# A token-mixing kernel: the last 64 tokens' products in pairs in the array's halves, and the bias on GpSimd

## The chip, the cores and the metric

The kernel runs on one core of a Trainium2 chip. The metric is the device time of one execution in microseconds (us). The engines are TensorE (PE in the profile; PEld is its loading of weights), VectorE (DVE), ScalarE (ACT), GpSimd (POOL) and SyncE (SP, which here only issues DMAs).

## The reference

Attention with pooled keys and values feeds a residual MLP block that first mixes tokens and then channels. Batch 8, 8 heads, 576 tokens, head size 64, so 512 channels:

```
k_p, v_p = means of k, v over groups of 8 tokens          # 72 of each
attn     = softmax(q k_p^T / 8) v_p                       # per batch and head, 576 x 64
x        = the heads side by side                         # 576 x 512
a1       = alpha1 * x + beta1
u        = x + lam * (w_tok a1)                           # w_tok 576 x 576: the "mix"
out      = u + lam * (relu((alpha2*u + beta2) w_ch1) w_ch2)
```

The mix is linear, so lam * (w_tok a1) is a product of w_tok with xs = lam*alpha1*x, plus a bias: the sum of each row of w_tok times lam*beta1.

## The kernel before

Tokens are cut in five chunks. Chunks 0 to 3 hold tokens 0 to 511 (token 4p+c is in partition p of chunk c); the last 64 tokens are the fifth, "chunk 4", and those of an even and an odd batch share one 128-partition chunk. All 36 chunks stand in a list in which four make a block of the MLP: nine blocks, n = 0 to 8. While PE works on the MLP of block n, the attention and the mix of batch n+1 are put between its products. The order on every engine is written out by hand: each step goes into the list `todo` with a place in time (`at`), the list is sorted, and the steps are issued in that order. Places 0 to 15 of a block are `mlp_A` (L838: first channel product, with a Relu on ACT), 16 to 31 the second product (`mlp_B` in blocks 0 and 1; from block 2 on `product`, L945, a Strassen-like form with seven products of half size, whose sums of operands are `hidden_sum`, L931, on DVE, and whose results `gather`, L976, adds up on DVE).

For each batch: `att_S4` (L689) makes the scores, with 64-row products in pairs in the array's two halves, and `exp` (L722) their exponentials on ACT into `ET`, whose last 64 columns beyond the tokens are kept at 1. `att_AV` (L733) multiplies by the values, and DVE divides (L749) and scales (L751) into `x_tm`, `x` for short, five columns of 128 tokens by 64 channels. Of the fifth, for the last 64 tokens, an even batch uses partitions 0 to 63 and an odd one 64 to 127. `att_X` (L761) multiplies by lam*alpha1 for two heads at a time into `xs_pool`, in bf16: four columns at L765, and the half column of the last tokens at L758 (`rest_X`). It runs on DVE, but for heads 4 and 5 on GpSimd.

`mix_T` (L794) makes one chunk of the mix with five products of 512 columns, four over 128 tokens each and one over the last 64 tokens. The bias is in that fifth product: row 64 of `xs` holds lam*beta1 and row 64 of the weights `wtT` the row sums of w_tok (odd batches: row 0, with the tokens in rows 64 to 127, and weights moved to column 5 of `wtT` by `setup_wtok_odd`). Chunk 4 of an odd batch makes both batches' last tokens, ten products with 64 columns of weights, in the array's column halves. DVE adds x (L805), ACT makes a bf16 copy (L809), and `mix_uT` (L813) transposes it by a DMA on SP's queue for the MLP.

PSUM is shared by two pools: `gp` (L218), six banks in turn, and two banks `ch`. GpSimd also sums keys (`sum_k`, L368), casts (`cast_rem`, L351) and issues some loads. What decides places around the mix, in batch b of block n = b-1:

```
at = 21.5 + 0.9 * c + 0.7 * (c == 4) if first else 21.0 + (1.3 if b == 2 else 1.15) * c
when = ((3, (4.6, 14.6)), (1, (8.6, 18.86)), (2, (8.8, 18.98)), (4, (22.3, 23.0)))   # hidden_sum
```

Of the kernel before, what the change touches and what calls it, by code (L numbers as in the profile page):

```python
# [188 lines left out]
def direct(  # L189
# [255 lines left out]
    for i in range(4):  # L445
        if i < 2:
            t = const.tile([SPG, 4, 66], F16, tag=f"vp1_{i}", name=f"vp1_{i}")
            nc.vector.memset(t, 8.0)
            vp1_pool.append(t)
            t = const.tile([P, 2, 4, SPG], BF, tag=f"kpT_{i}", name=f"kpT_{i}")  # L450
            nc.vector.memset(t, 0.0)
            kpT_pool.append(t)
            kp_pool.append(const.tile([P, 4, SPG], BF, tag=f"kp_{i}", name=f"kp_{i}"))
# [68 lines left out]
    def setup_rowsum(tcx):  # L522

        trc = P if tcx < 4 else REM
        cols = slice(P * tcx, P * tcx + trc)
        ps = gp("ps_rs")
        for sc in range(5):
            nc.tensor.matmul(out=ps[:, 0:trc], lhsT=ones_bf if sc < 4 else ones_lo,  # L528
                             rhs=wtT[:, sc, cols], start=(sc == 0), stop=(sc == 4))
        nc.scalar.copy(out=wtT[64:65, 4, cols], in_=ps[64:65, 0:trc])  # L530

    def setup_wtok_odd():
        nc.vector.memset(wtT[0:64, 5, 0:S], 0.0)
# [155 lines left out]
    def att_S4(b, u):  # L689

        st = st1[b]
        qT, kp, rest = st["qT"][u], kp_pool[u], st["rem_qT"]
        lo = [psB.tile([P, DM], FP, tag="ch", bufs=2, name="ps_s") for _ in range(2)]
        hi = [gp("ps_s") for _ in range(2)]
        r = [gp("ps_r")[0:SPG, 0:128].rearrange("p (h i) -> p h i", i=64) for _ in range(2)]

        def main(i):
            for a in range(2):
                rows = slice(64 * a, 64 * a + 64)
                nc.tensor.matmul(  # L700
                    out=(hi if i > 1 else lo)[a][0:SPG, 256 * (i % 2):256 * (i % 2) + 256],
                    lhsT=kp[rows, i, :], rhs=qT[rows, 2 * i:2 * i + 2, :])

        def rests(i):
            for a in range(2):
                rows = slice(64 * a, 64 * a + 64)
                nc.tensor.matmul(  # L707
                    out=r[a][:, i // 2], lhsT=kp[rows, i + a, :],
                    rhs=rest[rows, :, 2 * u + i // 2::4].rearrange("p c i -> p i c"))
# [12 lines left out]
        def exp(k):  # L722
            if k < 2:
                o, i = ET[:, k::2, 512:S], r[k]
            else:
                a, (pair, h) = k % 2, pairs[k // 2 - 1]
                o = ET[:, h:h + 2, 256 * a:256 * a + 256]
                i = pair[a][0:SPG, :].rearrange("p (h i) -> p h i", i=256)
            nc.scalar.activation(out=o, in_=i, func=AF.Exp, bias=0.0, scale=0.125)  # L729

        st["exp", u] = exp

    def att_AV(b, h):  # L733
        st = st1[b]
        if "x" not in st:
            st["x"] = st1[b - 1]["x"] if b % 2 else work.tile([P, 6, DM], FP, tag="x_tm", bufs=1, name="x_tm")
        ET, vp1, x = st["ET"][h], vp1_pool[h // 4], st["x"]
        ps_av = gp("ps_av")
        av = ps_av[:, 0:5 * 66].rearrange("p (c x) -> p c x", x=66)
        odd = b % 2  # L740
        for c in range(4):
            m0 = 256 * (c % 2) + 128 * (c // 2)
            nc.tensor.matmul(out=av[:, odd + c, :], lhsT=ET[:, m0:m0 + 128],  # L743
                             rhs=vp1[:, h % 4, :])

        r0 = 512 - 64 * odd
        nc.tensor.matmul(out=av[:, 4 - 4 * odd, :], lhsT=ET[:, r0:r0 + 128], rhs=vp1[:, h % 4, :])  # L747
        rec = recs[:, 8 * b + h]
        nc.vector.reciprocal(out=rec, in_=av[:, :, 64:65])  # L749
        dd = D * h  # L750
        nc.vector.tensor_tensor(out=x[:, 1 - odd:6 - odd, dd:dd + D], in0=av[:, :, 0:64],  # L751
                                in1=rec.unsqueeze(2).to_broadcast((P, 5, D)), op=ALU.mult)
# [8 lines left out]
    def att_X(b, h0, h1, eng=nc.vector, rest=True):  # L761

        x, xs = st1[b]["x"], xs_pool[b % 2]
        cols = slice(D * h0, D * h1)
        eng.tensor_tensor(  # L765
            out=xs[:, 0:4, cols], in0=x[:, 1:5, cols],
            in1=lamal_bc[:, cols].unsqueeze(1).to_broadcast((P, 4, D * (h1 - h0))), op=ALU.mult)
        if rest:
            rest_X(b, h0, h1, eng)
# [18 lines left out]
    def keep_warm(count):  # L788

        ps = psB.tile([P, DM], FP, tag="ch", bufs=2, name="ps_warm")  # L790
        for _ in range(count):
            nc.tensor.matmul(out=ps, lhsT=warm[:, 0:P], rhs=warm)  # L792

    def mix_T(b, c, eng=nc.vector):  # L794
        key, s = chunk_of(b, c)
        ps_tok = gp("ps_tok")
        parts = ((b % 2, 0, P),) if c < 4 else ((0, 0, 64), (1, 64, P))
        for sc in range(5):
            for i, p0, p1 in parts:
                kk, at = (P, sc) if sc < 4 else (P, 5) if i else (65, 4)  # L800
                nc.tensor.matmul(out=ps_tok[p0:p1], lhsT=wtT[0:kk, at, P * c:P * c + p1 - p0],  # L801
                                 rhs=xs_pool[i][0:kk, sc, :], start=(sc == 0), stop=(sc == 4))
# [95 lines left out]
    def scale_w2(g, i):  # L898

        if g not in w2l:  # L900
            if g == 1:
                both = const.tile([P, 6 * DM], BF, tag="vecs", name="w2_l")
                w2l[1] = both[:, 0:4 * DM].rearrange("p (i d) -> p i d", d=DM)
                wino["spare"] = both[:, 4 * DM:].rearrange("p (j t) -> p j t", t=HALF)
            else:
                w2l[g] = const.tile([P, 4, DM], BF, tag=("wt_bf", None, "w2_0", "w2_1")[g],
                                    name="w2_l")
        nc.vector.tensor_tensor(out=w2l[g][:, i], in0=w2[g][:, i], in1=lam_bc, op=ALU.mult)

# [166 lines left out]
    def attention(b):  # L1076
# [22 lines left out]
        for u in range(2):  # L1099
            at = (9.0 if first else 6.3, 13.6)[u]  # L1100
            todo.append((at, lambda u=u: att_S4(b, u)))
            for k, dt in enumerate((0.1, 0.1, 0.1, 0.7, 1.7, 1.75) if u else (0.1, 0.1, 0.1, 1.1, 2.1, 3.1)):
                todo.append((at + dt, lambda u=u, k=k: st1[b]["exp", u](k)))
            early = (5.7, 6.2, 4.2, 4.7) if first else (5.7, 6.2, 2.9, 3.4)
            for i, dt in enumerate((2.9, 3.4, 4.6, 5.1) if u else early):
                h = 4 * u + i
                todo.append((at + dt, lambda h=h: att_AV(b, h)))
                if i % 2:
                    eng = nc.gpsimd if h == 5 or first and h < 5 else nc.vector
                    todo.append((at + dt + 0.1, lambda h=h, eng=eng: att_X(b, h - 1, h + 1, eng)))  # L1110
        if first:
            for i, u in enumerate((0, 2, 1)):
# [4 lines left out]
            for i, at in enumerate(((0.2, 1.4, 2.2), (5.0, 7.2, 8.0))[u]):  # L1117
                todo.append((at, lambda u=u, i=i: att_V(b, u, 4 >> i)))
        for c in range(5):
            at = 21.5 + 0.9 * c + 0.7 * (c == 4) if first else 21.0 + (1.3 if b == 2 else 1.15) * c  # L1120
            if c < 4 or b % 2:
                todo.append((at, lambda c=c: mix_T(b, c)))
                key = (b, c) if c < 4 else (b - 1, 4)
                todo.append((at + (1.0 if first else 1.8), lambda key=key: mix_uT(key)))
        return todo

    for n in range(NBLK):
# [26 lines left out]
                todo.append((1.2 + g, lambda g=g: weight_sum(4, g)))  # L1154
        if n >= FIRST:
            last = n == NBLK - 1
            when = ((3, (4.6, 14.6)), (1, (8.6, 18.86)), (2, (8.8, 18.98)), (4, (22.3, 23.0)))
            if last:
                when = ((3, (4.6, 12.6)), (1, (8.6, 16.1)), (2, (8.8, 16.2)), (4, (18.6, 19.6)))
            for i, at in when:  # L1160
# [17 lines left out]
            else:  # L1178
                for m in range(4):
                    todo.append((27.2 if m < 2 else 29.2, lambda m=m: store(n, m)))  # L1180
        if n == 0:
            todo.append((6.2, lambda: setup_rowsum(4)))
            todo.append((8.3, setup_wtok_odd))
            for g in range(2, 4):
# [66 lines left out]
```

## Time and profile before

| what | value |
|---|---|
| median of 3 runs | 332.6 us (332.5 to 332.74) |
| the profiled execution | 332.3 us, span 330.6 us |
| granted TensorE clock | 1.000 |
| PE busy | 324.9 us, 98% |
| DVE, ACT, POOL busy | 235.5 us, 175.5 us, 95.6 us |
| the mix's products (L801) | 200, busy 44.9 us |
| starts of blocks 1 to 8 on PE | 67.55, 102.76, 137.68, 171.30, 206.21, 239.83, 274.74, 300.78 us |
| POOL's wait for x ahead of L765 | 108.6 us in 8 waits |

The span is the time from the first to the last instruction; the time beside it has 1.7 us more. A product is shown as rows x columns of the array that its weights take (64\*72 is half of the rows), then the rows and columns of what moves through. A record of a product lasts longer than its stream, so the times from start to start tell what a product costs PE. An even batch's block takes 33.6 us, an odd one's 34.9.

### The profile page before, as it was taken

How to read it: one execution, taken by the hardware profiler on the slowest of the kernel's cores; microseconds unless marked ns; L12 is line 12 of the kernel's file. 1: busy time of each engine (PE TensorE's matmuls, PEld its weight loads, DVE VectorE, ACT ScalarE, POOL GpSimd, SP SyncE). 2: the span in 40 equal slices, each digit the busy share in tenths (PEclk: the TensorE clock that was granted, in tenths of full speed). 3: DMA queues.
4: the chain of work that ended last, by engine and by line, in shares of the span. 5: the costliest groups of instructions: out<-in, count | busy, mean ns of one | idle time of the engine just before them, and what ended most of it. 6: DMA issues, size and time to landing. Idle time of an engine off the chain costs nothing.

```text
span 330.6 us, 6522 instructions
## 1 busy us (share of the span) xinstructions
PE 324.9 (98%) x2528; PEld 208.9 (63%) x2528; DVE 235.5 (71%) x490; ACT 175.5 (53%) x322; POOL 95.6 (29%) x110
## 2 busy tenths in 40 slices
PE   8999999999999999999999999999999999999995
PEld 3667764455545576656775677557755866586584
DVE  6674389999589969776967796878688783265263
ACT  2775989458323852387128812782268225803710
POOL 8769738301256011700290028102610200000000
PEclk9999999999999999999999999999999999999999
DMA  8999999959894982499549934995340044003003
GB/s 119 193 219 270 268 210 249 207 145 124 165 255 68 221 203 59 76 227 165 164 119 201 171 125 89 207 195 157 65 136 2 0 65 143 2 0 129 2 32 97
DMA packets 66618, 45.83 MB, mean 139 GB/s; under 512 B 34541, under 2 KB 57205, under 8 KB 66586
## 3 DMA queue, kind: packets, MB, share of 16 engines
q1 hardware_dynamic: 52236, 32.67, 42.6%
q0 software_dynamic: 13824, 12.40, 22.9%
q8 instruction: 20, 0.33, 0.4%
q10 hardware_dynamic: 526, 0.34, 0.3%
q14 instruction: 12, 0.10, 0.1%
HBM read 38.30 MB, written 9.44 MB: 144 GB/s over the span
## 4 chain that ended last, share of the span: by engine, by line
PE 98%; DVE 1%; issue 0%; ACT 0%
PE ps_h L849 38%; PE ps_w L972 26%; PE ps_tok L801 12%; PE ps_ch L869 8%; PE ps_av L743 3%; PE ps_s L700 2%; PE ps_warm L792 2%; PE ps_kp L632 1%; PE ps_r L707 1%; PE ps_av L747 1%; PE ps_q L589 1%; PE ps_sc L680 0%; PE ps_rs L528 0%; PE ps_w L516 0%; PE ps_uT L825 0%; PE ps_v L659 0%
## 5 line engine op out<-in xcount | busy, mean ns | idle before, releaser
L849 PE MATMUL ps_h<-u_fm,w 128*128 128x512 bf16 (+2 forms) x608 | 133.7, 369 | 0.2 <-DVE bias_cols L852 0.2
L856 ACT ACTIVATE H<-ps_h,bias_cols 128x512 bf16<-128x512 f32 x144 | 98.1, 688 | 56.5 <-PE ps_h L849 55.5
L849 PEld LDWEIGHTS <-w 128*128 128x128 bf16 x608 | 65.8, 114 | 49.7 <-issue 2.2
L972 PEld LDWEIGHTS <-H 128*128 128x128 bf16 x560 | 53.4, 98 | 10.9 <-DVE u_sb L990 1.2
L809 ACT CAST u_bf<-u_sb 128x512 bf16<-128x512 f32 x32 | 19.8, 618 | 70.0 <-issue 39.9
L972 PE MATMUL ps_w<-w_l,H 128*128 128x256 bf16 x448 | 53.6, 273 | 0.0
L990 DVE TENSOR_TENSOR u_sb<-u_sb,ps_w 128x512 f32<-128x512 f32 x54 | 36.3, 682 | 17.0 <-PE ps_w L972 17.0
L765 POOL TENSOR_TENSOR xs<-x_tm,lamal_bc 128x512 bf16<-128x512 f32 x12 | 15.9, 1330 | 108.8 <-DVE x_tm L751 108.6
L801 PE MATMUL ps_tok<-xs,wtT 128*128 128x512 bf16 (+3 forms) x200 | 44.9, 381 | 0.1
L805 DVE TENSOR_TENSOR u_sb<-x_tm,ps_tok 128x512 f32<-128x512 f32 (+1 forms) x40 | 27.3, 683 | 9.9 <-PE ps_tok L801 9.9
L751 DVE TENSOR_TENSOR x_tm<-ps_av,recs 128x320 f32<-128x320 f32 x64 | 31.5, 492 | 2.6
L729 ACT ACTIVATE ET<-ps_s 72x512 f16<-72x512 f32 x56 | 32.3, 591 | 0.0
L801 PEld LDWEIGHTS <-wtT 128*128 128x128 bf16 (+3 forms) x200 | 17.4, 100 | 16.2 <-issue 1.1
L749 DVE RECIPROCAL recs<-ps_av 128x5 f32<-128x5 f32 x64 | 12.1, 188 | 16.7 <-PE ps_av L747 16.6
L670 DVE TENSOR_TENSOR v_u<-v_u 72x1024 f32<-72x1024 f32 (+1 forms) x24 | 22.7, 948 | 0.2
L972 PE MATMUL ps_w<-w_t,h_s 128*128 128x256 bf16 x168 | 22.6, 273 | 0.0
L869 PEld LDWEIGHTS <-H 128*128 128x128 bf16 x128 | 11.9, 98 | 13.7 <-issue 0.4
L372 POOL TENSOR_TENSOR k_raw<-k_raw 128x512 f32<-128x512 f32 x14 | 18.7, 1338 | 1.2 <-PE ps_ch L869 0.7
L972 PEld LDWEIGHTS <-h_s 128*128 128x128 bf16 x168 | 16.4, 98 | 4.1
L941 DVE TENSOR_TENSOR H<-H,H 128x1024 bf16<-128x1024 bf16 x14 | 9.7, 690 | 12.8 <-ACT H L856 12.7
L374 POOL TENSOR_TENSOR k_bf<-k_raw 128x512 bf16<-128x512 f32 x14 | 18.5, 1318 | 1.1
L743 PEld LDWEIGHTS <-ET 72*128 72x128 f16 x256 | 14.0, 97 | 6.0 <-DVE vp L664 0.3
(153 smaller groups left out, 369.3 us busy)
## 6 DMA issues: line engine op xcount, KB each, us to landing
out_dram<-u_sb SPq DMA_DIRECT2D x29, 256.0 KB
k_raw<-in_k_dram SPq DMA_DIRECT2D x12, 512.0 KB
v_u<-in_v_dram SPq DMA_DIRECT2D x12, 512.0 KB
q_bf<-in_q_dram POOLq DMA_DIRECT2D x16, 256.0 KB, 7.4
w<-in_moe_w_ch_dram POOLq DMA_DIRECT2D x6, 512.0 KB, 12.9
out_dram<-u_sb SPq DMA_DIRECT2D x11, 128.0 KB
w<-in_moe_w_ch_dram POOLq DMA_DIRECT2D x1, 1024.0 KB, 14.3
k_raw<-in_k_dram POOLq DMA_DIRECT2D x2, 512.0 KB, 16.7
```

Source lines behind the costliest of these rows:

```text
L670: nc.vector.tensor_tensor(out=out, in0=t[:, :, 0:width], in1=t[:, :, width:2 * width], op=ALU.add)
L729: nc.scalar.activation(out=o, in_=i, func=AF.Exp, bias=0.0, scale=0.125)
L743: nc.tensor.matmul(out=av[:, odd + c, :], lhsT=ET[:, m0:m0 + 128], rhs=vp1[:, h % 4, :])
L751: nc.vector.tensor_tensor(out=x[:, 1 - odd:6 - odd, dd:dd + D], in0=av[:, :, 0:64], in1=rec.unsqueeze(2).to_broadcast((P, 5, D)), op=ALU.mult)
L801: nc.tensor.matmul(out=ps_tok[p0:p1], lhsT=wtT[0:kk, at, P * c:P * c + p1 - p0], rhs=xs_pool[i][0:kk, sc, :], start=(sc == 0), stop=(sc == 4))
L805: nc.vector.tensor_tensor(out=s["u"][p0:p1, :], in0=x[p0:p1, 1 + c if c < 4 else 5 - 5 * i, :], in1=ps_tok[p0:p1, 0:DM], op=ALU.add)
L809: nc.scalar.copy(out=s["u_bf"], in_=s["u"])
L849: nc.tensor.matmul(out=ps_h[:, t0:t1 + one], lhsT=w1_of(cc, j), rhs=rhs, start=(cc == 0), stop=(cc == 3))
L856: nc.scalar.activation(out=H4[n, j // 4][:, j % 4, :], in_=ps_h, func=AF.Relu, bias=bias_cols[:, j:j + 1], scale=1.0)
L869: nc.tensor.matmul(out=ps, lhsT=H_of(n, j)[:, 128 * m:128 * m + 128], rhs=(w2l if n else w2)[j // 4][:, j % 4, :], start=(j == 0), stop=(j ...
L972: nc.tensor.matmul(out=ps, lhsT=stat(j), rhs=moving(j), stop=(j == 7), start=(first and (pp == 0 or alone) and j == 0), skip_group_check=True)
L990: nc.vector.tensor_tensor(out=o, in0=o, in1=banks[key, "both"], op=ALU.add)
```

## The change

For the third batch on (b > 1; the first two stay as they are):

- `exp` writes the exponentials of the last 64 tokens twice, so `att_AV` gives them in both halves of the partitions, and `att_X` multiplies all five columns in one instruction of 640 elements per partition, on DVE for all heads.
- Chunks are mixed by `mix_in_pairs`. The products over the last 64 tokens of two chunks (0 and 1, 2 and 3) are issued together ahead of the first one's other products, one in rows 0 to 63 of the array and one in rows 64 to 127, each into its own bank. In chunk 4 the two batches' such products take rows 0 to 63 by columns 0 to 63 and rows 64 to 127 by columns 64 to 127.
- No bias is in the products. `bias_x` (row sums of w_tok times lam*beta1, bf16, for 128 channels at a time) is made once in block 0: five reductions on DVE (`sum_wtok`), one product `ps_row` that spreads lam*beta1 over the partitions, and twenty scaled copies on ACT (`setup_bias_x`). After `att_X` GpSimd adds it to x in place: one instruction of 640 for even batches, one of 512 and one of 128 for odd.
- Places move: the mix's chunks to 21.8 + 1.1 c (b = 2: 21.4 + 1.2 c), which puts chunks 2 to 4 one product later, `hidden_sum` 1's second half from 18.86 to 16.6, ahead of head 5, and `hidden_sum` 2's from 18.98 to 21.6, behind three gathers.
- Tiles are shared anew to make room for `bias_x`.

```diff
+    def sum_wtok(c):
+        p1 = P if c < 4 else REM
+        nc.vector.tensor_reduce(out=sums[0:p1, c:c + 1], in_=wt_bf[0:p1, S * c:S * c + S],
+                                op=ALU.add, axis=AX.X)
+        if c == 4:
+            nc.sync.dma_start(out=sums[64:128, 4:5], in_=sums[0:64, 4:5])
+    def setup_bias_x(hp, c):
+        if not ps_row:
+            ps_row.append(gp("ps_row"))
+            nc.tensor.matmul(out=ps_row[0], lhsT=ones_bf[64:65], rhs=xs_pool[0][64:65, 4, :])
+        if c == 0:
+            bias_x.append(wino["spare0"] if hp == 3 else const.tile(
+                [P, 5, 2 * D], BF, tag=("kpT_0", "kpT_1", "vs16")[hp], name="bias_x"))
+        nc.scalar.activation(out=bias_x[hp][:, c], in_=ps_row[0][:, 2 * D * hp:2 * D * hp + 2 * D],
+                             func=AF.Copy, bias=0.0, scale=sums[:, c:c + 1])
...
-            if k < 2:
+            if k < 2 and b < 2:
                 o, i = ET[:, k::2, 512:S], r[k]
+            elif k < 2:
+                o = ET[:, k::2, 512:].rearrange("p h (n i) -> p h n i", i=64)
+                i = r[k].unsqueeze(2).to_broadcast((SPG, 2, 2, 64))
...
-        r0 = 512 - 64 * odd
+        r0 = 512 if b > 1 else 512 - 64 * odd
...
+        if b > 1:
+            x = x[:, 1 - b % 2:6 - b % 2, cols]
+            eng.tensor_tensor(
+                out=xs[:, :, cols], in0=x, op=ALU.mult,
+                in1=lamal_bc[:, cols].unsqueeze(1).to_broadcast((P, 5, D * (h1 - h0))))
+            bias = bias_x[h0 // 2]
+            for x, bias in ((x[:, 1:5], bias[:, 0:4]), (x[:, 0:1], bias[:, 4:5])) if b % 2 else (
+                    (x, bias),):
+                nc.gpsimd.tensor_tensor(out=x, in0=x, in1=bias, op=ALU.add)
+            return
...
+    def mix_in_pairs(b, c, parts):
+        if c % 2 == 0:
+            for k in range(2):
+                i, p0, p1 = parts[k] if c == 4 else parts[0]
+                cc = c if c == 4 else c + k
+                if k == 0 or c < 4:
+                    mixed[b, cc] = gp("ps_tok")
+                rows = slice(64 * k, 64 * k + 64)
+                nc.tensor.matmul(out=mixed[b, cc][p0:p1],
+                                 lhsT=wtT[rows, 4 + k, P * cc:P * cc + p1 - p0],
+                                 rhs=xs_pool[i][rows, 0 if i else 4, :], start=True, stop=False)
+        for sc in range(4):
+            for i, p0, p1 in parts:
+                nc.tensor.matmul(out=mixed[b, c][p0:p1], lhsT=wtT[:, sc, P * c:P * c + p1 - p0],
+                                 rhs=xs_pool[i][:, sc + i, :], start=False, stop=(sc == 3))
...
-                    eng = nc.gpsimd if h == 5 or first and h < 5 else nc.vector
+                    eng = nc.gpsimd if first and h < 6 else nc.vector
...
-            at = 21.5 + 0.9 * c + 0.7 * (c == 4) if first else 21.0 + (1.3 if b == 2 else 1.15) * c
+            at = (21.5 + 0.9 * c + 0.7 * (c == 4) if first else
+                  21.4 + 1.2 * c if b == 2 else 21.8 + 1.1 * c)
...
-            when = ((3, (4.6, 14.6)), (1, (8.6, 18.86)), (2, (8.8, 18.98)), (4, (22.3, 23.0)))
+            when = ((3, (4.6, 14.6)), (1, (8.6, 16.6)), (2, (8.8, 21.6)), (4, (22.3, 23.0)))
...
+            for c in range(5):
+                todo.append((8.35 + 0.1 * c, lambda c=c: sum_wtok(c)))
+                for hp in range(4):
+                    todo.append((26.3 + hp + 0.2 * c, lambda hp=hp, c=c: setup_bias_x(hp, c)))
```

More of the change, by code (lines that the diff above doesn't have):

```diff
@@ L449, in direct @@
             vp1_pool.append(t)
-            t = const.tile([P, 2, 4, SPG], BF, tag=f"kpT_{i}", name=f"kpT_{i}")
+            t = const.tile([P, 640], BF, tag=f"kpT_{i}", name=f"kpT_{i}")
+            t = t[:, 0:8 * SPG].rearrange("p (a h g) -> p a h g", a=2, h=4)
             nc.vector.memset(t, 0.0)
@@ L530, in setup_rowsum @@
         nc.scalar.copy(out=wtT[64:65, 4, cols], in_=ps[64:65, 0:trc])
+    sums = const.tile([P, 5], FP, tag="sums", name="sums")
+    bias_x = []
+    def sum_wtok(c):
[4 more added lines that the diff above has]
+            nc.sync.dma_start(out=sums[64:128, 4:5], in_=sums[0:64, 4:5])
+    ps_row = []
+    def setup_bias_x(hp, c):
[7 more added lines that the diff above has]
+                             func=AF.Copy, bias=0.0, scale=sums[:, c:c + 1])
     def setup_wtok_odd():
@@ L792, in keep_warm @@
             nc.tensor.matmul(out=ps, lhsT=warm[:, 0:P], rhs=warm)
+    mixed = {}
+    def mix_in_pairs(b, c, parts):
[13 more added lines that the diff above has]
+                                 rhs=xs_pool[i][:, sc + i, :], start=False, stop=(sc == 3))
     def mix_T(b, c, eng=nc.vector):
         key, s = chunk_of(b, c)
-        ps_tok = gp("ps_tok")
         parts = ((b % 2, 0, P),) if c < 4 else ((0, 0, 64), (1, 64, P))
[L798 to L802, printed above, removed]
+        if b > 1:
+            mix_in_pairs(b, c, parts)
+            ps_tok = mixed.pop((b, c))
+        else:
+            ps_tok = gp("ps_tok")
+            for sc in range(5):
+                for i, p0, p1 in parts:
+                    kk, at = (P, sc) if sc < 4 else (P, 5) if i else (65, 4)
+                    nc.tensor.matmul(out=ps_tok[p0:p1],
+                                     lhsT=wtT[0:kk, at, P * c:P * c + p1 - p0],
+                                     rhs=xs_pool[i][0:kk, sc, :], start=(sc == 0), stop=(sc == 4))
         for i, p0, p1 in parts:
@@ L904, in scale_w2 @@
                 wino["spare"] = both[:, 4 * DM:].rearrange("p (j t) -> p j t", t=HALF)
+            elif g == 0:
+                both = const.tile([P, 5 * S + 64], BF, tag="wt_bf", name="w2_l")
+                w2l[0] = both[:, 0:4 * DM].rearrange("p (i d) -> p i d", d=DM)
+                wino["spare0"] = both[:, 4 * DM:4 * DM + 640].rearrange("p (c d) -> p c d", c=5)
             else:
-                w2l[g] = const.tile([P, 4, DM], BF, tag=("wt_bf", None, "w2_0", "w2_1")[g],
+                w2l[g] = const.tile([P, 4, DM], BF, tag=(None, None, "w2_0", "w2_1")[g],
                                     name="w2_l")
```

## The prediction

> **What bounds the kernel now.** I read the page's busy shares and chain first, then what TensorE (PE) waited for, then the timeline of PE at the places that the change touches, then VectorE (DVE) just ahead of the mix.
>
> ```profile
> PE 324.9 (98%) x2528; PEld 208.9 (63%) x2528; DVE 235.5 (71%) x490; ACT 175.5 (53%) x322; POOL 95.6 (29%) x110
> PE 98%; DVE 1%; issue 0%; ACT 0%
> ```
>
> ```profile
> PE ps_warm L792 <- DVE early L413: 1.4, 1, 1.4
> PE ps_h L849 <- DVE bias_cols L852: 0.2, 1, 0.2
> ```
>
> PE is busy throughout and is the whole chain; its waits add up to 1.6 us, all ahead of 30 us. So only fewer PE microseconds can win, and no later wait is there to be removed. Other engines matter where they come late for PE.
>
> What does a product in half the array cost? The scores' products (L700, L707) already run in such pairs. Timeline of PE in the block of the fifth batch (b=4):
>
> ```profile
> 151.12 0.60 PE L849 MATMUL ps_h<-u_fm,w 128*128 128x512 bf16 x2
> 151.65 0.30 PE L700 MATMUL ps_s<-qT,kp 64*72 64x256 bf16 x2
> ...
> 151.85 0.39 PE L700 MATMUL ps_s<-qT,kp 64*72 64x256 bf16 x4
> 152.08 0.24 PE L707 MATMUL ps_r<-rem_qT,kp 64*72 64x64 bf16 x2
> 152.15 0.28 PE L700 MATMUL ps_s<-qT,kp 64*72 64x256 bf16 x2
> 152.36 1.92 PE L849 MATMUL ps_h<-u_fm,w 128*128 128x512 bf16 x8
> ```
>
> Unbroken, a whole-array product of 512 columns takes 0.216 us (five mix products from 159.98 to 161.06) and one of 256 takes 0.109 (eight L972 from 161.06 to 161.93). Four half-array products of 256 take 0.23 us (151.85 to 152.08), so the halves do run two at once. But at both borders PE loses time with nothing to wait for. Two L849 products from 151.12 end at 151.55; the first half starts 0.10 later. The last two halves start at 152.15, stream 0.107, and the next product starts at 152.36: 0.10 lost. The eight after it take 1.76 until the next line at 154.12, against 1.73: the first after a border costs 0.03 more. Borders into and out of the mix's 64-column products show the same:
>
> ```profile
> 200.54 1.04 PE L972 MATMUL ps_w<-w_t,h_s 128*128 128x256 bf16 x8
> 201.50 1.27 PE L801 MATMUL ps_tok<-xs,wtT 128*64 128x512 bf16 x10
> 202.71 1.05 PE L972 MATMUL ps_w<-w_l,H 128*128 128x256 bf16 x8
> ```
>
> Eight of 0.109 end at 201.41, the next starts at 201.50; ten products in column halves then take five streams (1.08) plus 0.12 until 202.71.
>
> **The change, part by part.** The sum is made on the profiled execution: 332.3 us (span 330.6, 1.7 around it); the median shown is 332.6, 0.3 above it, and I add the sum to the median.
>
> *Pairs.* Each batch from the third on has two pairs (chunks 0/1 and 2/3), 12 in six batches. A pair replaces two products (0.432) by: border 0.10, first-after-border 0.03, one stream 0.216, border back 0.10, first product after it 0.03: 0.476. Net +0.04, not -0.216. Six second pairs: +0.25. (The first pairs are with the wait, below.)
>
> The Trainium skill (TensorEngine Tiling (Array Packing), Key Properties) says that a change of tiling mode drains TensorE. The trace agrees, with 0.10 us at each border. By that page's Theoretical Speedup (twice for a contraction of 64 or less) the 12 pairs would save 2.6 us.
>
> *Chunk 4* (odd batches, three of them). Before, its last-token products were already two at once, in column halves. Now they are in two quarters (64 rows by 64 columns), followed by the eight in column halves: nothing saved, and one border more, 0.13 each, if quarters-to-halves counts as a border. No row shows that: below 0.13 down to 0 if it doesn't; up to 0.35 if the two quarters, which write one bank, also go one after the other (0.216). I take 0.13, since every change of shape in the trace costs it: +0.39.
>
> The Trainium skill (same page, Gotcha 1: PSUM Pressure) says that different row tiles can't access one PSUM bank at the same time. That would give the 0.35, +0.65 over three batches; no run here shows it.
>
> *ps_row.* One more 512-column product with one row, in block 0: 0.10+0.03+0.216+0.10+0.03 = +0.48; between 0.22 (no borders) and 0.52.
>
> *The wait at the mix.* Before, GpSimd (POOL) multiplied heads 4-5 (L765) and DVE only 6-7, then came `hidden_sum` 1. Odd batch b=5:
>
> ```profile
> 188.97 0.20 DVE L749 RECIPROCAL recs<-ps_av 128x5 f32<-128x5 f32 x1 [1.52 <-PE ps_av L747]
> 189.27 0.49 DVE L751 TENSOR_TENSOR x_tm<-ps_av,recs 128x320 f32<-128x320 f32 x1
> 190.00 0.19 DVE L749 RECIPROCAL recs<-ps_av 128x5 f32<-128x5 f32 x1 [0.24 <-PE ps_av L747]
> ...
> 191.03 0.19 DVE L749 RECIPROCAL recs<-ps_av 128x5 f32<-128x5 f32 x1 [0.31 <-PE ps_av L747]
> ...
> 192.41 0.74 DVE L765 TENSOR_TENSOR xs<-x_tm,lamal_bc 128x512 bf16<-128x512 f32 x1
> 193.18 0.29 DVE L758 TENSOR_TENSOR xs<-x_tm,lamal_bc 64x128 bf16<-64x128 f32 x1
> 193.50 0.69 DVE L941 TENSOR_TENSOR H<-H,H 128x1024 bf16<-128x1024 bf16 x1
> ```
>
> ```profile
> 193.60 0.38 PE L801 MATMUL ps_tok<-xs,wtT 128*128 128x512 bf16 x1
> ```
>
> PE reaches the mix at 193.60; the first four parts of xs are done at 193.15, a margin of 0.45. The instruction order of the changed program puts two more things on DVE in this stretch: `hidden_sum` 1 (0.60 from start to start) between heads 4 and 5, and the multiplication for heads 4-5. The new multiplications are 640 wide: 0.74 plus a quarter of a 72x512 step (1.21-0.68 = 0.53 more for 512) = 0.87. DVE's chain: scale 4 at 189.27, hidden sum 189.68, division 5 190.28, scale 190.50 to 190.99, xs(4-5) 191.03, division 6 191.78, scales to 193.12, xs(6-7) 193.15 to 194.02, handed over by 194.05. The first pair needs the fifth part, so all of it. PE waits 0.45, with all its later work queued behind. The same working gives 0.34 in the even batches b=4, 6 (xs at 160.27, PE there at 159.98) and 0.20 for b=2 (no hidden sum there; 89.95 against 89.80). Sum 3 x 0.45 + 2 x 0.34 + 0.20 = 2.23. The border into the first pair lies inside this wait, so that pair is 0.376 against 0.432: -0.34 for six. Net +1.89. Bounds: 0, if DVE were 0.45 quicker than worked out; +3.0 more (five batches by 0.6), if the hidden sum meets POOL: the like-typed L929 ran 1.30 us with POOL beside it and 0.68 without. I take neither: POOL's add for heads 2-3 should be over by 188.7, a microsecond before the hidden sum.
>
> *At nothing.* POOL's bias adds: about 1.27 + 0.45 us (its L765, L758) four times a batch, in POOL's idle 17.3 us ahead of 190.80; the last runs from 194.05 to 195.9, while DVE has three gathers and a hidden sum (2.4 us) ahead of the first `u` addition, so DVE doesn't wait. Behind the adds on POOL queue `cast_rem` and `sum_k`, done 4.5 us before their products; uncovered, each lost microsecond would be one of PE. Five reductions on DVE in block 0: 0.49 at 320 wide, by slope some 0.7 start to start at 576, 3.5 in all, in DVE's idle 3.50 ahead of 39.82 (and one small DMA on SP, idle there); uncovered, they would delay that cast, which scores at 44.33 need. Twenty ACT copies: 0.17 start to start, 3.5 us, in ACT's idle 3.07 ahead of 68.62; the first Relu is 0.5 late, covered by PE's six banks (0.86 us each). Exponentials of 256 instead of 128 columns: +0.2 us per four heads, in ACT's 0.18 waits. The chunks mixed one product later reach the transposes on SP's queue some 1.5 us later, with `att_Frem` now ahead of one (1.2 us); the tightest, 132.38 for 137.68, keeps over 3 us; 0 to 1 us in one block.
>
> Sum: 0.25 + 0.39 + 0.48 + 1.89 = +3.0; 332.6 + 3.0 = 335.6, forecast 335.5.
>
> **The rivals.**
> - *Halves without borders* (faster). If a lone pair cost one stream: 12 x 0.216 = 2.6 saved, 0.22 for ps_row, no waits: 330.2. For it: halves start together. Against: 0.10 at every border in the trace. It decides where a round trip costs under 0.216; the rows say 0.26.
> - *One border hidden, no wait.* 0.13 a pair: -1.0, +0.35 for ps_row, +0.2 for chunk 4: 332.1, the same. Against: both sides are seen.
> - *Borders, but no wait at the mix.* All 12 pairs +0.5, chunk 4 +0.39, ps_row +0.48: 334.0. For it: 0.45 us is small, and DVE's idle 0.24 and 0.31 between heads may absorb more than I counted.
> - *A worse meeting.* The hidden sum beside POOL's adds (half of 3.0) or quarters one after the other (+0.65): 336.2 to 338.6. For it: L929's 1.30.
>
> **How the numbers follow.** Forecast 0.55 (335.5), no wait 0.17, worse 0.15, same 0.07, faster 0.06. Faster by over 0.2% (0.7 us, about what this kernel's measurement can tell) 0.06, within it 0.07, slower 0.87. The range runs from the no-wait case with chunk 4 at its low end (333.5) to one part of the worse case (337.3).
>
> **What would show it.** In the changed profile: PE gaps of 0.10 on both sides of each 64x512 pair, starts 0.13 apart behind chunk 4's quarters, a PE wait of 0.2 to 0.5 on DVE's xs ahead of each batch's first pair, some 0.5 around ps_row, and L929-like long hidden sums only if POOL meets them. Pairs followed at once by the next product would prove me wrong, as would a first pair that finds xs ready.

## The result, and the profile after

The changed kernel takes 336.98 us (median of 5 runs, 336.39 to 338.03) against 332.54 us (332.29 to 332.74): ratio 1.0138, 95% interval 1.0117 to 1.0159. The forecast was 335.5, range 333.5 to 337.3. So the sign was right and the size was 1.5 us short. The profiled execution is the longest of the five (338.03 us, span 336.3), which matters below. Single executions, of the kernel before too, had a granted clock of 0.98 to 0.995 instead of 0.997 to 1.000 and took 1 to 4 us longer; they are the high ends of the ranges of ten and twelve runs below.

The page's busy shares and its chain, after the change:

```profile
PE 323.9 (96%) x2498; PEld 206.7 (61%) x2529; DVE 243.5 (72%) x483; ACT 182.3 (54%) x342; POOL 122.4 (36%) x134
PE 76%; DVE 13%; DMA 3%; ACT 3%; POOL 2%; issue 2%; POOLq 0%; ACTq 0%; DVEq 0%
```

PE's busy time, as recorded, has not grown, but PE is no longer the whole chain: VectorE stands in it with 13%. (31 of PE's product records are missing here, as the counts 2498 and 2529 show; a place where two starts lie 0.43 instead of 0.216 apart, with nothing to wait for, is such a hole.) What PE waits for, longest first:

```profile
PE ps_tok L843 <- DVE xs L795: 1.9, 6, 0.4
...
PE ps_s L725 <- DVE x_tm L779: 0.7, 1, 0.7
...
PE ps_r L732 <- ACT H L918: 0.3, 1, 0.3
```

The first line is the wait that the prediction named, in all six batches. The wait for `x_tm` (L779) and the one for ACT's Relus (L918) were not in its sum. The mix of the batch whose VectorE lines the prediction showed (b=5), VectorE first, then PE:

```profile
193.44 0.68 DVE L1007 TENSOR_TENSOR H<-H,H 128x1024 bf16<-128x1024 bf16 x1
...
194.78 0.82 DVE L795 TENSOR_TENSOR xs<-x_tm,lamal_bc 128x640 bf16<-128x640 f32 x1
...
196.89 1.01 DVE L795 TENSOR_TENSOR xs<-x_tm,lamal_bc 128x640 bf16<-128x640 f32 x1
```

```profile
194.81 2.79 PE L1038 MATMUL ps_w<-w_l,H 128*128 128x256 bf16 x24
197.96 0.39 PE L843 MATMUL ps_tok<-xs,wtT 64*128 64x512 bf16 x2 [0.37 <-DVE xs L795]
...
201.76 1.04 PE L1038 MATMUL ps_w<-w_t,h_s 128*128 128x256 bf16 x8
202.73 0.39 PE L843 MATMUL ps_tok<-xs,wtT 64*128 64x512 bf16 x2
203.06 1.04 PE L848 MATMUL ps_tok<-xs,wtT 128*128 128x512 bf16 x4
```

The hidden sum (L1007) and both 640-wide multiplications stand in VectorE's row as worked out, and the last ends at 197.90. PE's 24 products end their streams at 197.43; the first pair starts at 197.96, 0.53 later. The border into it lies inside this wait: in `whole_rows` below, where there is no border, the first product waits just as long. The second pair waits for nothing: eight products from 201.76 end at 202.63, the pair starts at 202.73 and the next product at 203.06 (0.10, one stream of 0.216, 0.11), and the product after that comes 0.01 later than without a border. That is 0.43 in all. Two whole-array products take 0.432. The pair gains nothing.

Where the time went can be added up without any hole in the records from ScalarE's 144 Relus, since both kernels have the same ones in the same order. The table gives, for every traced kernel, by how much PE's work falls behind the profile of before in each stretch (difference of a Relu's start to that of the same Relu before the change, and of that again from stretch to stretch), us:

| kernel | to the first Relu | blocks 0 and 1 | mix b=2 | each mix b=3, 5, 7 | each mix b=4, 6 | end | span in all |
|---|---|---|---|---|---|---|---|
| changed | +0.20 | +2.65 | +0.17 | +0.55 | +0.27 | +0.54 | +5.73 |
| `bias_early` | -0.35 | +1.47 | +0.17 | +0.55 | +0.27 | +0.41 | +3.91 |
| `hidden_back` | +0.03 | +1.93 | +0.17 | +0.35 | +0.07 | +0.18 | +3.51 |
| `one_trip` | +0.13 | +1.58 | +0.21 | +0.33 | +0.06 | +0.13 | +3.16 |
| `whole_rows` | +0.17 | +1.58 | +0.29 | +0.54 | +0.38 | +0.42 | +4.84 |
| `scale_later` | +0.06 | +0.43 | +0.17 | +0.55 | +0.27 | +0.43 | +3.29 |
| `no_add_b2` | -0.39 | +1.09 | +0.06 | +0.57 | +0.27 | +0.83 | +3.84 |
| `attx_pool` | -0.05 | +1.92 | -0.03 | +0.11 | -0.03 | +0.41 | +2.53 |
| `all_mended` | +0.38 | +0.22 | +0.20 | +0.02 | -0.15 | +0.89 | +1.46 |
| `all_mended_x` | -0.34 | +0.27 | +0.01 | -0.22 | -0.24 | +0.03 | -1.18 |
| `mended_again` | -0.23 | +0.70 | +0.00 | -0.22 | -0.24 | +0.02 | -0.65 |
| `no_row` | +0.09 | +4.46 | +0.01 | -0.22 | -0.24 | +0.05 | +3.45 |

The first and the last column are start-up loads and the landing of the last stores; they differ by up to 0.9 between kernels whose code there is alike, so they are taken as the spread of single executions. The mix columns repeat to 0.01. The mixes cost 2.36 in all (0.17 + 3 x 0.55 + 2 x 0.27) where the prediction had 2.53. Blocks 0 and 1 cost 2.65 where it had 0.48. There lies the miss.

### The profile page after: what moved, and what is told of

It is laid out like the page before. It is cut to its first block, busy times and chain, and to the rows that moved or that the text cites. A ratio compares the mean times of both kernels' runs of the same rounds, so it can differ in the third digit from the quotient of the medians.

```text
span 336.3 us, 6525 instructions
## 1 busy us (share of the span) xinstructions
PE 323.9 (96%) x2498; PEld 206.7 (61%) x2529; DVE 243.5 (72%) x483; ACT 182.3 (54%) x342; POOL 122.4 (36%) x134
## 4 chain that ended last, share of the span: by engine, by line
PE 76%; DVE 13%; DMA 3%; ACT 3%; POOL 2%; issue 2%; POOLq 0%; ACTq 0%; DVEq 0%
PE ps_h L911 34%; PE ps_w L1038 19%; PE ps_tok L848 7%; PE ps_ch L931 5%; DVE x_tm L779 4%; DVE xs L795 3%; DMA wt_bf<-in_moe_w_tok_dram 3%; PE ps_s L725 2%; PE ps_tok L862 2%; DVE w_l L974 2%; PE ps_tok L843 2%; PE ps_av L771 1%; DVE recs L777 1%; ACT bias_x L554 1%; ACT H L918 1%
## 5 line engine op out<-in xcount | busy, mean ns | idle before, releaser
L918 ACT ACTIVATE H<-ps_h,bias_cols 128x512 bf16<-128x512 f32 x144 | 97.7, 696 | 45.0 <-PE ps_h L911 44.0
L801 POOL TENSOR_TENSOR x_tm<-x_tm,bias_x 128x640 f32<-128x640 f32 (+2 forms) x27 | 28.7, 1075 | 89.8 <-DVE xs L795 83.2
L779 DVE TENSOR_TENSOR x_tm<-ps_av,recs 128x320 f32<-128x320 f32 x64 | 31.5, 492 | 2.3
L848 PE MATMUL ps_tok<-xs,wtT 128*128 128x512 bf16 (+1 forms) x115 | 26.8, 381 | 0.8 <-issue 0.8
L795 DVE TENSOR_TENSOR xs<-x_tm,lamal_bc 128x640 bf16<-128x640 f32 x24 | 20.5, 856 | 0.8
L1007 DVE TENSOR_TENSOR H<-H,H 128x1024 bf16<-128x1024 bf16 x14 | 9.6, 688 | 12.4 <-ACT H L918 12.4
L266 POOL DMA_DIRECT2D q_bf<-in_q_dram x16 | 12.5, 787 | 14.2 <-DVE v_u L345 13.3
```

The costliest lines, as they stand in the source:

```text
L795: eng.tensor_tensor(out=xs[:, :, cols], in0=x, op=ALU.mult, in1=lamal_bc[:, cols].unsqueeze(1).to_broadcast((P, 5, D * (h1 - h0))))
L801: nc.gpsimd.tensor_tensor(out=x, in0=x, in1=bias, op=ALU.add)
L848: nc.tensor.matmul(out=mixed[b, c][p0:p1], lhsT=wtT[:, sc, P * c:P * c + p1 - p0], rhs=xs_pool[i][:, sc + i, :], start=False, stop=(sc == 3))
L918: nc.scalar.activation(out=H4[n, j // 4][:, j % 4, :], in_=ps_h, func=AF.Relu, bias=bias_cols[:, j:j + 1], scale=1.0)
```

## The experiments

All start from the changed kernel unless said otherwise. Four questions: what a trip into halves costs, what makes the first pair wait, what blocks 0 and 1 lose, and whether anything is left when all that is mended.

**A trip into halves.** `one_trip` puts both pairs of a batch behind one border:

```diff
-        if c % 2 == 0:
-            for k in range(2):
+        if c in (0, 4):
+            for k in range(2 if c else 4):
...
-                cc = c if c == 4 else c + k
+                cc = c if c == 4 else k
...
-                rows = slice(64 * k, 64 * k + 64)
+                rows = slice(64 * (k % 2), 64 * (k % 2) + 64)
```

> The two pairs of a batch run one behind the other, ahead of chunk 0, so that six trips into halves and back are left instead of twelve. Theory 'a border is paid for each trip, whatever is inside': six times 0.10 + 0.10 + 0.02 = 1.3 less, 335.7, and inside a trip the second pair starts 0.216 after the first. Rival 'each pair costs by itself' (the halves share what they stream): no change, 337.0. Rival 'four banks taken at once': PE waits for a bank in front of the second pair, 0.2 or more in each batch, 337 or slower.

336.74 us (335.47 to 337.05), ratio to before 1.0116 (1.0082 to 1.0151). The time alone decides nothing here, the table does: 0.22 less in each odd and 0.21 less in each even batch, which is one trip (0.10 + 0.11). The timeline of PE at b=5, in `one_trip`:

```profile
196.45 0.60 PE L843 MATMUL ps_tok<-xs,wtT 64*128 64x512 bf16 x4 [0.37 <-DVE xs L795]
196.99 1.04 PE L848 MATMUL ps_tok<-xs,wtT 128*128 128x512 bf16 x4
```

Four half-array products take 0.54 from first start to next product: two streams and one border out. A border is paid for each trip, whatever is inside. In b=2 the gain is lost again: PE loses 0.25 behind the next block's first scores, where it lost nothing with two trips.

`whole_rows` takes the halves away and leaves all else (two rows of the weights are cleared, so that the products over all rows are the same sums):

```diff
+            todo.append((26.0, lambda: nc.gpsimd.memset(wtT[64:65, 4, :], 0.0)))
+            todo.append((26.0, lambda: nc.gpsimd.memset(wtT[0:1, 5, :], 0.0)))
...
-                rows = slice(64 * k, 64 * k + 64)
-                nc.tensor.matmul(out=mixed[b, cc][p0:p1],
-                                 lhsT=wtT[rows, 4 + k, P * cc:P * cc + p1 - p0],
-                                 rhs=xs_pool[i][rows, 0 if i else 4, :], start=True, stop=False)
+                for i, p0, p1 in parts:
+                    nc.tensor.matmul(out=mixed[b, cc][p0:p1],
+                                     lhsT=wtT[:, 4 + (i if c == 4 else 0), P * cc:P * cc + p1 - p0],
+                                     rhs=xs_pool[i][:, 0 if i else 4, :], start=True, stop=False)
```

> The products over the last 64 tokens use all rows again (the other half of the weights is zero, two rows of the weights are cleared for it), one for each chunk, and chunk 4 runs in column halves throughout; the bias stays on GpSimd and VectorE's order is that of the changed kernel. Theory 'a lone pair of 512 columns gains nothing for its two borders': first pairs 0.216 + 0.10 against 0.432 whole, six times 0.1 slower; second pairs 0.42 against 0.432, no difference; chunk 4 three times 0.12 faster; sum +0.3, 337.3. Theory 'pairs save what they leave out, and the loss is all elsewhere': twelve products of 0.216 come back, 339.6.

337.22 us (336.83 to 337.81), ratio 1.0129 (1.0093 to 1.0166). Even batches lose 0.11 more than with pairs, odd ones 0.01 less (0.11 against chunk 4's 0.12). The theory that pairs save their 0.216 each, 2.6 in all, falls: six batches without a pair cost 0.3 more in sum. The first product waits as before:

```profile
197.09 0.61 PE L840 MATMUL ps_tok<-xs,wtT 128*128 128x512 bf16 x2 [0.37 <-DVE xs L795]
```

So the wait belongs to VectorE's order, not to the halves.

**What the first pair waits for.** `hidden_back` gives the two hidden sums their old places:

```diff
-            when = ((3, (4.6, 14.6)), (1, (8.6, 16.6)), (2, (8.8, 21.6)), (4, (22.3, 23.0)))
+            when = ((3, (4.6, 14.6)), (1, (8.6, 18.86)), (2, (8.8, 18.98)), (4, (22.3, 23.0)))
```

> Only the two hidden sums go back to their places of before (18.86 and 18.98), behind the last multiplication for xs. Theory 'the hidden sum stands in front of xs': VectorE's chain ahead of the mix is 0.6 us shorter from the fourth batch on, the first pair's loss of 0.43 (odd batches, border of 0.10 not counted) and 0.29 (even) goes, that of the third batch (0.41) stays: 3 x 0.43 + 2 x 0.29 = 1.9 less, 335.1. Rival 'the wait is the 640 wide multiplications of VectorE': a third to a half of it stays, 335.8. Rival 'the sum then meets GpSimd's additions': it takes 1.3 us instead of 0.7, the fourth product waits for it, 336 to 337.

335.85 us (335.82 to 336.59), ratio 1.0094 (1.0058 to 1.0129). The rival with VectorE's wide multiplications was the right one: 0.20 less in every batch from b=3 on, not the 0.43 and 0.29 that were expected. At b=5 the idle time ahead of the first pair is 0.17 instead of 0.37:

```profile
196.50 0.39 PE L843 MATMUL ps_tok<-xs,wtT 64*128 64x512 bf16 x2 [0.17 <-DVE xs L795]
```

The sum takes 0.6 from start to start, but without it VectorE waits for PE's heads again (0.31 ahead of head 5), so only 0.2 of it lay on the path. The last multiplication still takes 1.01 instead of 0.82: GpSimd's short addition (0.42) began 0.1 ahead of it. `attx_pool` has the same edit and gives the multiplication of heads 4 and 5 back to GpSimd:

```diff
-                    eng = nc.gpsimd if first and h < 6 else nc.vector
+                    eng = nc.gpsimd if h == 5 or first and h < 5 else nc.vector
```

> The hidden sums at their old places, and in addition the multiplication of heads 4 and 5 back on GpSimd in all batches. Theory 'the rest of the wait at the first pair is this multiplication on VectorE': against the version with the hidden sums alone the wait of 0.24 (odd batches), 0.10 (even) and 0.20 (third) goes, 1.1 less: block starts +0.11 in odd, -0.03 in even batches against before, time 334.8. Rival 'GpSimd's two additions of the bias come later by 1.6 us, so VectorE's addition of u waits for them and PE for a bank': as much is lost behind the mix, 336 or slower.

334.80 us (333.64 to 336.50, 10 runs), ratio 1.0059 (1.0041 to 1.0078). The mixes are as expected to the hundredth: +0.11 in odd and -0.03 in even batches. No line of PE waiting for `xs` is left in its mixes from b=2 on. GpSimd's later additions cost nothing there: the rival falls. So of what the first pair of an odd batch lost by waiting, 0.20 was the hidden sum, and 0.24 went with heads 4 and 5.

Not all of these 0.24 are VectorE's own work. In the changed kernel the last multiplication, the one that the first pair waits for, begins in every batch while one of GpSimd's additions runs. It takes 1.01 in odd batches, 0.87 in even ones and 0.94 in b=2; all others take 0.82 to 0.83. In `attx_pool` it begins just ahead of the addition from b=3 on and takes 0.82 to 0.83 as well. So that edit took away two things at once. GpSimd and VectorE at b=2 in the changed kernel:

```profile
90.80 1.40 POOL L801 TENSOR_TENSOR x_tm<-x_tm,bias_x 128x640 f32<-128x640 f32 x1 [3.05 <-DVE recs L777]
...
91.94 0.94 DVE L795 TENSOR_TENSOR xs<-x_tm,lamal_bc 128x640 bf16<-128x640 f32 x1
```

The run `no_add_b2` below leaves out this batch's additions. There the same multiplication takes 0.82 too:

```profile
89.80 0.82 DVE L795 TENSOR_TENSOR xs<-x_tm,lamal_bc 128x640 bf16<-128x640 f32 x1
```

PE then stands 0.19 ahead of the first pair of b=2, against 0.30 in `bias_early` (the changed kernel's trace has a hole there), and the mix of b=2 costs 0.06 instead of 0.17. For the other batches the price (0.19 in odd ones, 0.05 in even ones) is read from the durations; no run left out their additions alone. In sum the additions make up 0.8 us of the six waits.

**Blocks 0 and 1.** One part of their 2.65 is `ps_row`: 0.31 from its start to the next and 0.10 ahead of it, 0.42, as predicted within 0.06. Of the rest, the trace shows two suspects in block 1. First VectorE and GpSimd in the changed kernel, near 82 us:

```profile
81.85 1.93 DVE L974 TENSOR_TENSOR w_l<-w,lam_bc 128x512 bf16<-128x512 bf16 x1
83.70 0.18 DVE L777 RECIPROCAL recs<-ps_av 128x5 f32<-128x5 f32 x1
```

```profile
81.83 1.39 POOL L801 TENSOR_TENSOR x_tm<-x_tm,bias_x 128x640 f32<-128x640 f32 x1 [3.49 <-DVE v_u L345]
```

```profile
84.46 0.30 PE L725 MATMUL ps_s<-qT,kp 64*72 64x256 bf16 x1 [0.65 <-DVE x_tm L779]
```

GpSimd starts its first addition of the bias 0.02 ahead of a scaling of w2 (`scale_w2`), which then takes 1.93. Before the change it took 0.69:

```profile
80.20 0.69 DVE L908 TENSOR_TENSOR w_l<-w,lam_bc 128x512 bf16<-128x512 bf16 x1
```

The division behind it comes late, and the scores wait for the bank that it frees. `scale_later` moves that one scaling behind the division:

```diff
-            for piece, at in enumerate((0.5, 2.6, 5.2, 8.4, 10.9, 13.3)):
+            for piece, at in enumerate((0.5, 2.6, 5.2, 8.4, 12.7, 13.3)):
```

> One scaling of w2 on VectorE in the second block moves from ahead of the division of heads 0 and 1 to behind it (10.9 to 12.7); all else is the changed kernel (336.98). Theory 'GpSimd's addition of the bias makes this scaling take 1.93 us instead of 0.69, the division comes late and the second group of scores waits for its bank': the losses of 0.7 and 0.2 behind 83.54 go, 336.1, and the scaling takes 0.7. Rival 'the division is late because PE's own scores were late, or because the 640 wide multiplication is longer': the wait stays, 337.0.

336.54 us (335.69 to 338.12), ratio 1.0125 (1.0100 to 1.0150): four runs too wide apart for half a microsecond. In its profiled run (335.69) blocks 0 and 1 lose 0.43, which is `ps_row` alone, against 1.58 in `one_trip` and `whole_rows`, whose code in this place is that of the changed kernel: 1.15 gained where 0.9 was expected. But the scaling did not take 0.7: one of the two now behind the division takes 1.89, since GpSimd's next addition stands beside it, and nobody waits for it there. The move shows where the time is lost, not that GpSimd is the cause. `no_add_b2` shows that. It leaves out the addition of the bias for the third batch:

```diff
+            if b == 2:
+                return
             bias = bias_x[h0 // 2]
```

> The changed kernel, but in the third batch GpSimd adds no bias (this part of the computation is left out). Theory 'GpSimd's addition makes VectorE's scaling of w2 take 1.93 us': the scaling at 81.85 takes 0.69 in its old place, and the PE losses of 0.7 and 0.2 behind 83.54 go without any move. Rival 'the scaling merely stands in the wrong place, or the 640 wide multiplication is the delay': the loss stays. Time 336.0 in the first case, 337.0 in the second, the trace decides.

336.15 us (one run). VectorE and PE in the same place:

```profile
80.84 0.69 DVE L976 TENSOR_TENSOR w_l<-w,lam_bc 128x512 bf16<-128x512 bf16 x1
```

```profile
82.43 0.39 PE L725 MATMUL ps_s<-qT,kp 64*72 64x256 bf16 x4
...
82.73 0.28 PE L725 MATMUL ps_s<-qT,kp 64*72 64x256 bf16 x2
```

The scaling takes 0.69 in its old place and the scores run through. GpSimd's addition is the cause of the 1.15.

The second suspect are the twenty copies on ScalarE ahead of the first Relu. In the changed kernel:

```profile
66.56 0.62 ACT L871 CAST u_bf<-u_sb 128x512 bf16<-128x512 f32 x1 [4.61 <-DVE u_sb L867]
67.09 3.97 ACT L554 ACTIVATE bias_x<-ps_row,sums 128x128 bf16<-128x128 f32 x15
70.84 1.51 ACT L554 ACTIVATE w_l<-ps_row,sums 128x128 bf16<-128x128 f32 x5
72.08 1.41 ACT L918 ACTIVATE H<-ps_h,bias_cols 128x512 bf16<-128x512 f32 x2
```

They take 0.25 from start to start (20 from 67.09 to 72.08), and the first Relu starts 3.5 later than the 68.62 of before. The cast ahead of them came at 64.94 then, and it waited for VectorE too:

```profile
64.94 0.62 ACT L809 CAST u_bf<-u_sb 128x512 bf16<-128x512 f32 x1 [3.19 <-DVE u_sb L805]
```

`bias_early` moves copies and `ps_row` into ScalarE's idle time ahead of the cast:

```diff
-                    todo.append((26.3 + hp + 0.2 * c, lambda hp=hp, c=c: setup_bias_x(hp, c)))
+                    todo.append((25.31 + 0.1 * hp + 0.02 * c, lambda hp=hp, c=c: setup_bias_x(hp, c)))
```

> The twenty scaled copies and the product with one row move ahead of the last mix chunk of the second batch, into the 4.6 us in which ScalarE had nothing to do; all else is as in the changed kernel (336.98). Theory 'the copies make the first Relu late': the waits of PE for a bank that the Relus release (0.20 at 72.64, 0.13 at 74.95 and 0.45 at 75.29 in the changed profile) go, the first Relu starts at 69 to 70 instead of 72.08, 336.2. Rival 'ScalarE is late only because VectorE's scaling was (3.97 instead of 2.55 us), the copies are hidden': nothing changes, 337.0. Rival 'all that the second block loses hangs on ScalarE': also the wait of 0.8 at 83.54 goes, 335.2.

336.44 us (336.31 to 337.69), ratio 1.0117 (1.0078 to 1.0155). The first Relu starts at 68.60, the waits in front of the first scores are gone, and the one of 0.8 near 82 stays: blocks 0 and 1 lose 1.47, `ps_row` and the scaling. What the copies cost in their old place can be read from the kernels that left them there. Counted from each run's own start-up (first column of the table taken off), with the first Relu at 70.40, 70.41 and 70.78 they cost nothing (`whole_rows`, `scale_later`, `one_trip`: 1.58, 0.43 and 1.58 are `ps_row` with or without the scaling), at 71.15 and 71.17 they cost 0.35 (`attx_pool`, `hidden_back`), at 71.48 0.67 (`no_add_b2`), at 71.88 1.08 (the changed kernel). So PE's six banks cover the lateness up to 70.8, 2.2 us behind the 68.62 of before, and from there it costs one for one. How late the copies start differs between executions. In the profiled run of the changed kernel GpSimd waited 1.4 us for a load of k, and its `sum_k` behind it met the four scalings of w2 (3.97 us in all, 2.55 before) ahead of the addition that the cast waits for. The 1.08 are thus partly that execution's own.

**All of it mended.** `all_mended` joins these edits, except GpSimd's heads 4 and 5, with chunk 4 in column halves throughout (the two rows cleared as above) and `ps_row` as a product over 65 rows:

```diff
-            nc.tensor.matmul(out=ps_row[0], lhsT=ones_bf[64:65], rhs=xs_pool[0][64:65, 4, :])
+            nc.tensor.matmul(out=ps_row[0], lhsT=ones_lo[0:65], rhs=xs_pool[0][0:65, 4, :])
...
+            for half in range(2):
+                todo.append((7.0, lambda k=half: nc.gpsimd.memset(ones_lo[64 * k:64 * k + 64], k)))
```

> All single edits together: copies ahead of the last mix chunk, hidden sums at their old places, one trip for both pairs, chunk 4 in column halves throughout, the scaling behind the division, and the row for the bias as a product of 65 rows (64 of weight zero), so without borders. By the terms measured one by one against the changed kernel (336.98): -0.3 (row) -0.9 (scaling) -0.4 (ScalarE, its middle) -1.0 (hidden sums, five times 0.2) -1.3 (one trip) -0.35 (chunk 4) = -4.25, 332.7: no different from the kernel before (332.5). If the terms share a wait, 333.5.

333.10 us (332.79 to 336.76, 12 runs), ratio 1.0018 (0.9998 to 1.0039): no different from the kernel before, and 0.4 from the sum of the single terms. `ps_row` costs 0.22 without borders. `all_mended_x` adds heads 4 and 5 on GpSimd:

> The same with heads 4 and 5 on GpSimd. If the rest of the wait goes with it (0.24, 0.10 and 0.20 a batch, 1.1 in all): a batch then has one trip of 0.20 and two streams of 0.216 in place of four, 0.23 less, 1.4 in six batches, against 0.22 for the row: 331.4, faster than before by 0.3%. If VectorE's additions wait for GpSimd's instead: 333 or slower.

331.54 us (331.13 to 335.62, 12 runs) against 332.94 beside it, ratio 0.9974 (0.9943 to 1.0004), and a second time, as `mended_again`:

> The version with all edits and heads 4 and 5 on GpSimd once more, since its interval of [0.9943, 1.0004] held one. Theory 'its block starts fall 0.24 a batch behind those of the kernel before, less 0.26 in the second and 0.25 in the third block': 0.9 less, 331.6 against 332.5, interval below one. If the difference was that of the chip alone: a ratio of 1.0.

331.85 us (331.12 to 335.86, 12 runs) against 332.74, ratio 0.9967 (0.9927 to 1.0006). Both medians are 0.9 to 1.4 us below the kernel before. Both intervals, which go by means, still hold one; but 16 of the 24 runs are shorter than the shortest of the 46 runs of the kernel before beside them (332.20 us), so a gain of about 1 us is seen in the times too. The traces have it where it was summed up: 0.22 to 0.24 less in each mix from b=3 on, in both executions. (`mended_again` lost 0.4 more at the start of block 1, where PE waited 0.3 for a transposed chunk. `all_mended_x`, with the same code, had no such wait; the cause is open.) PE at b=5 in `all_mended_x`, without a wait:

```profile
190.45 2.79 PE L1041 MATMUL ps_w<-w_l,H 128*128 128x256 bf16 x24
193.17 0.61 PE L847 MATMUL ps_tok<-xs,wtT 64*128 64x512 bf16 x4
193.71 1.04 PE L851 MATMUL ps_tok<-xs,wtT 128*128 128x512 bf16 x4
```

`no_row` tried to save the last 0.22 by loading beta1 to all partitions and scaling it on GpSimd:

> The version with all edits and heads 4 and 5 on GpSimd, and in addition no product for the bias row: beta1 is loaded to all partitions by one DMA of 256 KB, GpSimd multiplies it by lambda, and ScalarE's twenty copies read it from SBUF. If the row's product costs PE its 0.22 and nothing else changes: block starts in sum 1.1 below the kernel before, 331.3 against its 332.5, ratio 0.9965. If the load or the multiplication is late for the copies, they are late for the Relus again: 332.

335.42 us (334.31 to 338.62, 12 runs), ratio 1.0043 (0.9996 to 1.0090): the rival, and worse than it had put it. The load landed only at 65.9 us, and GpSimd stood waiting for it with its key sums behind:

```profile
65.92 1.43 POOL L551 TENSOR_TENSOR row_bc<-row_bc,lam_bc 128x512 f32<-128x512 f32 x1 [12.68 <-DMA row_bc<-in_moe_beta_dram]
```

Copies, keys and Relus came late one after the other, and blocks 0 and 1 lost 4.46.

## Why the prediction came out 1.5 us short

Step by step, measured values from the table and the changed kernel's trace:

| step | predicted | measured |
|---|---|---|
| second pairs, six | +0.25 | -0.02 (0.43 for 0.432) |
| first pairs with their wait | +1.89 | +2.03 (mixes 2.36, less the rows above and below); 0.8 of it are GpSimd's additions, mostly by durations |
| chunk 4, three | +0.39 | +0.35 (0.12 each) |
| `ps_row` | +0.48 | +0.42 |
| GpSimd's additions elsewhere | 0 | +1.15, in block 1 |
| copies on ScalarE | 0 | 0 to +1.1, by execution |
| sum | +3.0 | +3.9 to +5.0; median of the runs +4.4 |

- *Borders.* Right: 0.10 on both sides. The separate 0.03 for the first product behind a border was counted too high (0.01 here). So a lone pair is even rather than 0.04 dearer. The faster rival named the point from which it decides, a round trip under 0.216: measured 0.21, of which nothing is left.
- *Chunk 4.* Quarters to column halves is a border (0.12), and the two quarters run at once: from their start to the next product 0.33, against 0.32 for a pair in two banks. PE of the changed kernel at b=7:

```profile
275.98 0.40 PE L843 MATMUL ps_tok<-xs,wtT 64*64 64x512 bf16 x2
276.31 1.05 PE L848 MATMUL ps_tok<-xs,wtT 128*64 128x512 bf16 x8
```

  One after the other would be 0.55. The Trainium skill (TensorEngine Tiling (Array Packing), Gotcha 1: PSUM Pressure) says that different row tiles can't access one PSUM bank at the same time; these two write different partitions of one bank, and the measurement decides: no serialisation here.
- *The wait.* Predicted, with the border inside, 0.45, 0.34 and 0.20 for odd batches, even ones and b=2. (For the last two the times given differ by 0.29 and 0.15 only; the other 0.05 have no source.) Measured from the end of PE's streams to the first pair: 0.53, 0.39 and 0.30. The path was right, and the hidden sum's part in it was shown. But the six waits are 0.4 us longer than worked out, with 0.8 us of GpSimd's additions in them, and the borders, cheaper than thought, take 0.3 back. That this term came out within 0.2 is partly luck.
- *"GpSimd's bias adds" at nothing.* This step failed. It asked whether GpSimd has time for them and whether VectorE waits for their result, and both answers held. It did not ask what they do to VectorE's instructions beside them, although the prediction used the row that shows it (L929, 1.30 us beside GpSimd, a mean of six from 0.69 to 1.76, and 0.68 without) and kept it for the hidden sum in a rival. The hidden sum met nothing (0.68). The last multiplication for xs, which the wait was worked out from, met an addition in every batch; and the scaling of w2 in the third batch's block, which the prediction never named, met one and cost 1.15.
- *"Twenty copies" at nothing.* The price was wrong (0.17 from start to start in the sum, 0.25 measured, 5.0 us instead of 3.5), and so was the margin: ScalarE's idle 3.07 ahead of 68.62 starts only when a cast is done that itself waits for VectorE. Predicted 0.5 late for the first Relu, measured 1.8 to 3.3, counted as above; the banks covered 2.2.

The rival of "a worse meeting" (336.2 to 338.6) thus holds the result, with its mechanism right and its place wrong.

## What to carry to other kernels

A trip into another tiling shape of the array has a fixed price, here 0.21 us for both borders, and a pair of 512 columns saves 0.216: lone pairs are worth nothing, and the first step is to put several behind one border. Before an operation is given to an idle engine, look not only for time on that engine but for what runs beside it on the other engine, and whether that is waited for; a row of the old trace that is long for its shape tells the price. When a preparation is put "into idle time", read what ended that idle time, and whether what ended it can itself come late.

## What the runs showed of the hardware that was not expected

- A VectorE instruction with both operands in SBUF and an addition on GpSimd do not run side by side: one stands until the other is done, by order of start. At 81.83 GpSimd began first: its addition took its 1.39, and the scaling, begun 0.02 later, ended 0.56 after it. The last multiplication for xs (0.82 alone) ended 0.68 after the addition that it met, in every batch from b=2 on. At 85.81 VectorE began first: the scaling took 0.69, and GpSimd's addition, begun at 85.97, took 1.78. VectorE's additions of `u`, with one operand in PSUM, take 0.67 to 0.69 with GpSimd beside them or not (14 and 18 of them in the changed kernel). The Trainium skill (SBUF — State Buffer, Who interferes with whom) says this of a VectorE instruction with two SBUF inputs and a GpSimd instruction that reads SBUF: whichever issues first has the shared port for the whole instruction. The trace agrees with its order of issue and with its exception for one SBUF input.
- ScalarE's copies of 128x128 out of PSUM with a scale per partition start 0.25 us apart when nothing waits.
- With four banks taken at once the mix of b=2 lost 0.25 in the next block, in the traced execution of each of the five kernels with one trip. In `all_mended_x` the product goes on at 110.79, as an exponential that empties a bank of scores ends (110.19 and 0.59 long): a bank's turn, perhaps, but no run tested it.
